# Four weight blocks instead of two share one row of 256-column products in the first token group of a two-layer MLP kernel

## The chip, the core and the metric

The kernel runs on one NeuronCore of one Trainium2 chip. The metric is the device time of one execution in microseconds, median of several executions. Five engines matter here: PE (TensorE, the matrix products), DVE (VectorE) and ACT (ScalarE) for elementwise work, SP for the DMA queue, and the DMA engines. Each engine works through its own list of instructions in the order in which the program issued them, and waits at an instruction until the semaphores that it needs have arrived.

## The reference

Attention with a sigmoid in place of the softmax, then two MLP layers, all in fp32:

```python
scores = scale * np.matmul(q, k.transpose(0, 1, 3, 2)) - np.log(S)
x = np.matmul(1.0 / (1.0 + np.exp(-scores)), v)      # 4 x 12 x 448 x 64 -> 1792 x 768
h = x @ w_in1; r = np.maximum(h, 0.0)                # 768 -> 2048
x = (s * (r * r) + b) @ w_out1                       # 2048 -> 768
h = x @ w_in2
g = np.maximum(h, 0.0) + alpha * np.minimum(h, 0.0)
out = g @ w_out2
```

The weights arrive as 64-bit floats and are turned into fp32 on the chip.

## The kernel before

After the attention (the first 131 us) the two MLP layers run as six passes, three token groups for each of the two layers: `PASSES`, (m, p). Group p = 0 has 768 tokens, groups 1 and 2 have 512. The first group therefore exists twice, as pass 0 and as pass 3, and the change touches these two passes alone.

A pass is 34 steps (`PER`), one weight block ("unit") each, numbered r = 0 to 33. Units 0 to 15 are "in": each makes one 128-row block of h out of six x blocks (six terms). Units 16 to 33 are "out": six output blocks dc, each cut into three units of 6, 5 and 5 terms (`OUT_CUTS`), which add into one accumulator; unit 16 reads g[0..5], unit 17 g[6..10], unit 18 g[11..15], and unit 19 is the first of the next output block.

Every fp32 operand is split into a high and a low part of a reduced precision, since a product of full precision is made of three: high x high, high x low, low x high. Per term and unit, `products` (L396) issues for p = 0: three products of 512 columns (L411 to L413), one of 512 columns that covers the last 256 tokens' high and low part with the high weight (L416), and one of 256 columns with the low weight (L402, the "short" one). The short ones of one unit stand in a row: an even unit has its row last, an odd unit its row first (`short_first`), so that the rows of units 2k and 2k+1 join to one row of 12 (or 11, or 10).

A step (loop at L564) issues, in this order: the stores of earlier steps, the products of unit n on PE, then the handling of the sums of unit n-1 (`evac`), then `split_unit(n+2)`, then `fetch(n+5)`, and in some steps a load or split of the next pass's x.

- `evac` of an "in" unit in group 0: ACT copies the sums out of PSUM (L437), DVE adds the second short part (L439), two more DVE operations (L447, L454 in layer 1; L461, L465 in layer 2), ACT casts the high part of g (L210), DVE subtracts for the low part (L217, two instructions). Of an "out" unit only the last cut of a block is handled (L437, L439 and a store).
- `split_unit(n+2)`: ACT casts the high part of the weights (L99), DVE subtracts for the low part (L102). Four buffers (`whl`).
- `fetch(n+5)`: either a load, or, for the units in `JUST` (the out units of pass 0 and 3), a conversion from 64 bits: ACT L141, DVE L147, L152, L155. So in passes 0 and 3 the steps 11 to 28 each carry a conversion.

Sums lie in PSUM in two pools of two buffers (`acc` for even blocks, `av` for odd ones), so unit k+4 takes the place of unit k.

Of the kernel before, what the change touches and what calls it, by code (L numbers as in the profile page):

```python
# [12 lines left out]
ALU = mybir.AluOpType  # L13
# [3 lines left out]
P = 128  # L17
OUT_CUTS = [(0, 6), (6, 11), (11, 16)]

PASSES = [(0, 0), (0, 1), (0, 2), (1, 0), (1, 1), (1, 2)]  # L20
N5 = 512
# [15 lines left out]
def tile_kernel(  # L37
# [13 lines left out]
    nc = tc.nc  # L51
    B, NPR, _, SKQ = kq.shape
# [3 lines left out]
    NK = NPR  # L56
    DM = NK * P
    NFC = w_in1.shape[0]
# [5 lines left out]
    TG = N5 + REST  # L64
    TOK = [TG, N5, N5]
    TOK0 = [0, TG, TG + N5]
    NCUT = len(OUT_CUTS)
    PER = NFC + NK * NCUT
# [22 lines left out]
    def t_tile(name):  # L91
        return tp.tile([P, TG], F32, tag="t", name=name)
# [4 lines left out]
    def split(hi, lo, src, eng_hi):  # L97
        if eng_hi == "A":
            nc.scalar.copy(hi, src)  # L99
        else:  # L100
            nc.vector.tensor_copy(hi, src)
        nc.vector.tensor_tensor(out=lo, in0=src, in1=hi.bitcast(F32), op=ALU.subtract)  # L102
# [17 lines left out]
    uses = [m * PER + j for m, _ in PASSES for j in range(PER)]  # L120
    r64, w32, wraw, whl = {}, {}, {}, {}
# [39 lines left out]
    def store32():  # L161
        for j, w in to_store:
            n = units[j][1]
            w32[j] = dram.tile([P, n], F32, tag=f"w{j}", name=f"w{j}")
            nc.sync.dma_start(out=w32[j], in_=w[:, :n])
        to_store.clear()

    def wraw_tile():
        return wrawp.tile([P, WMAX], F32, tag="wraw", name="wraw")

    def load32(i):
        n = units[uses[i]][1]
        t = wraw_tile()
        nc.sync.dma_start(out=t[:, :n], in_=w32[uses[i]])
        wraw[i] = t

    def split_unit(i):
        if i >= len(uses):
            return
        n = units[uses[i]][1]  # L180
        t = whlp.tile([P, 2, WMAX], F32R, tag="whl", name="whl")
        split(t[:, 0, :n], t[:, 1, :n], wraw.pop(i)[:, :n], "A")
        whl[i] = t
# [8 lines left out]
    def next64():  # L192
        if at64[0] < len(order64):
            load64(order64[at64[0]])
            at64[0] += 1


    x, x_dram, xr = {}, {}, {}
# [132 lines left out]
    def flush_stores():  # L331
        for dst, t in stores:
            nc.sync.dma_start(out=dst, in_=t)
        stores.clear()
# [6 lines left out]
    for _ in range(NWARM):  # L341
        for h in range(2):
            for j in range(2):
# [3 lines left out]
                    start=True, stop=True,  # L347
# [16 lines left out]
    for u in range(NU + 2):  # L364
# [7 lines left out]
        if u >= 2:  # L372
            q, c = order[u - 2]
# [5 lines left out]
        if u in conv_step:  # L379
            k = conv_step[u]  # L380
            w = ga[k][:, :WMAX]
# [11 lines left out]

    g, hp, op_ = {}, {}, {}

    def products(dst, p, terms, first, last, short_first):  # L396

        n = len(terms) - 1

        def short(start, stop):  # L400
            for k, (hi, lo, mv) in enumerate(terms):
                nc.tensor.matmul(  # L402
                    dst[:, N5:TG], lo, mv[:, 2 * N5 : N5 + TG],
                    start=start and k == 0, stop=stop and k == n, skip_group_check=True,
                )

        if p == 0 and short_first:
            short(first, False)
        for k, (hi, lo, mv) in enumerate(terms):
            end = last and k == n  # L410
            nc.tensor.matmul(dst[:, :N5], hi, mv[:, N5 : 2 * N5], start=first and k == 0, stop=False)  # L411
            nc.tensor.matmul(dst[:, :N5], hi, mv[:, :N5], start=False, stop=False)  # L412
            nc.tensor.matmul(dst[:, :N5], lo, mv[:, N5 : 2 * N5], start=False, stop=end)  # L413
        if p == 0:
            for k, (hi, lo, mv) in enumerate(terms):
                nc.tensor.matmul(  # L416
                    dst[:, N5 : 2 * N5], hi, mv[:, 2 * N5 :],
                    start=first and not short_first and k == 0,
                    stop=last and short_first and k == n,
                    skip_group_check=True,  # L420
                )
            if not short_first:
                short(False, last)

    def in_mm(p, fc, i):
        hp[fc] = (acc_tile, av_tile)[fc % 2]("hps").rearrange("p b s -> p (b s)")
        w = whl.pop(i)
        terms = []
        for kc in range(NK):
            cols = slice(kc * P, (kc + 1) * P)  # L430
            terms.append((w[:, 0, cols], w[:, 1, cols], x[kc]))
        products(hp[fc], p, terms, True, True, i % 2 == 1)

    def take(h, p, name):

# [39 lines left out]
        g[fc] = g_tile(fc).bitcast(F32R)[:, : 2 * TG]  # L475
        split_to(g[fc], t, 0, "A" if p == 0 else "V")

    def out_mm(p, dc, cut, i):
        c0, c1 = OUT_CUTS[cut]
        if c0 == 0:  # L480
            op_[dc] = (acc_tile, av_tile)[dc % 2]("ops").rearrange("p b s -> p (b s)")
        w = whl.pop(i)
        if i == len(uses) - 1:


            M = N5 // 2
            t = t_tile("o")[:, :N5]
            o2 = (acc_tile, av_tile)[(dc + 1) % 2]("ops2").rearrange("p b s -> p (b s)")
            for h in range(2):
                to = op_[dc] if h == 0 else o2  # L490
                for fc in range(c0, c1):
                    cols = slice((fc - c0) * P, (fc - c0 + 1) * P)
                    for k, o in ((0, N5), (0, 0), (1, N5)):
                        nc.tensor.matmul(  # L494
                            to[:, :M], w[:, k, cols],
                            g[fc][:, o + h * M : o + (h + 1) * M],
                            start=h == 1 and fc == c0 and k == 0 and o == N5,
                            stop=fc == c1 - 1 and k == 1,
                        )
                if h == 0:  # L500
                    nc.scalar.copy(t, op_[dc][:, :N5])
                else:
                    nc.vector.tensor_tensor(  # L503
                        out=t[:, M:], in0=o2[:, :M], in1=t[:, M:], op=ALU.add
                    )
                c = TOK0[p] + h * M
                nc.sync.dma_start(
                    out=out[dc * P : (dc + 1) * P, c : c + M], in_=t[:, h * M : (h + 1) * M]
                )
            return  # L510
        terms = []
        for fc in range(c0, c1):
            cols = slice((fc - c0) * P, (fc - c0 + 1) * P)
            terms.append((w[:, 0, cols], w[:, 1, cols], g[fc]))
        products(op_[dc], p, terms, c0 == 0, c1 == NFC, i % 2 == 1)

    def out_evac(m, p, dc):
        t = take(op_.pop(dc), p, "o")
        if m == 0:
            dst = x_store(1, p, dc)  # L520
        else:
            dst = out[dc * P : (dc + 1) * P, TOK0[p] : TOK0[p] + TOK[p]]
        stores.append((dst, t))

    def load_xr(key):
        xr[key] = t_tile("xr")[:, : TOK[key[1]]]
        nc.sync.dma_start(out=xr[key], in_=x_dram[key])

    def make_x(key):
        split_to(x_tile(key[2]), xr.pop(key), 0, "A")  # L530

    def evac(st):
        kind, m, p, c, cut = st
        if kind == "in":
            in_evac(m, p, c)
        elif cut == NCUT - 1:
            out_evac(m, p, c)

    def fetch(i):

        if i >= len(uses) or i in wraw:
            return
        j = uses[i]
        if j in JUST and j not in w32:
            w = wraw_tile()
            convert(j, w, "A")
            next64()
            wraw[i] = w
        else:
            load32(i)  # L550

    steps = []
# [6 lines left out]

    ahead = {PER + 2 + 4 * k: PER + k for k in range(NFC)}  # L560

    n_split, n_fetch = 2, 5
    pend = None
    for n, st in enumerate(steps):  # L564
        kind, m, p, c, cut = st
        o, r = divmod(n, PER)
        flush_stores()
        store32()
        if kind == "in":
            in_mm(p, c, n)  # L570
        else:
            out_mm(p, c, cut, n)
        if pend is not None:
            evac(pend)
        pend = st
        while n_split <= n + 2:
            split_unit(n_split)
            fetch(n_fetch)
            n_split += 1
            n_fetch += 1  # L580
        if kind == "out" and o + 1 < len(PASSES):

            kc, odd = divmod(r - NFC - 3, 2)
            if 0 <= kc < NK:
                key = (*PASSES[o + 1], kc)
                if odd:
                    make_x(key)
                else:
                    load_xr(key)
        if n in ahead:  # L590
            convert(ahead[n], t_tile("cw"), "A")
            next64()
# [42 lines left out]
```

## Time and profile before

| what | us |
|---|---|
| median of 3 runs | 1054.35 (1053.59 to 1054.69) |
| the profiled execution, its time | 1053.89 |
| its span, first to last instruction | 1052.1 |
| PE busy | 1047.9 |
| DVE busy | 594.8 |
| ACT busy | 448.5 |

The profile's page lists engines, slices of the span, DMA queues, the chain of work that ended last, and the costliest groups of instructions. Of a matmul the start is recorded and the end is modelled, so rows of matmuls are read from start to start: the time between the starts of two stretches is what the first one took. "idle before" in brackets is the time that the engine stood still ahead of an instruction, with what ended it.

### The profile page before, as it was taken

Reading aid. Unit: us, or ns where it says so; the run is one execution under the profiler, and the core shown is the slowest. Engines: PE = TensorE matmul, PEld = TensorE weight load, DVE = VectorE, ACT = ScalarE, POOL = GpSimd, SP = SyncE. Lnnn points to the kernel's source line nnn. Section 1 sums busy time; section 2 is a strip of 40 time slices with the busy share of each in tenths; the row PEclk is TensorE's granted clock in tenths of the full one; section 3 lists DMA queues with packets and bytes.
Section 4 is the critical chain, followed back from the end, with each engine's and each line's share of the span. In section 5 each row is a group of like instructions: output and inputs, shape, how many; then the busy total and the mean of one; then the engine's idle time right before and its main releaser. Section 6 shows DMA issues by size and latency. Waiting matters only on the chain.

```text
span 1052.1 us, 14275 instructions
## 1 busy us (share of the span) xinstructions
PE 1047.9 (100%) x5631; PEld 818.3 (78%) x5631; DVE 594.8 (57%) x881; ACT 448.5 (43%) x625; POOL 0.2 (0%) x4
## 2 busy tenths in 40 slices
PE   9999999999999999999999999999999999999998
PEld 4333388888888888888888888888888888888887
DVE  4765456687643775447745366786616652266521
ACT  6777733444332554335534333443314432344321
POOL 0000000000000000000000000000000000000000
PEclk9999999999999999999999999999999999999999
DMA  7787660048762545764566512468523235323330
GB/s 276 274 268 248 244 249 1 27 140 262 250 225 93 195 138 203 270 207 136 183 220 207 187 61 60 120 187 291 201 93 105 89 122 170 130 90 98 116 117 31
DMA packets 62131, 173.17 MB, mean 165 GB/s; under 512 B 8048, under 2 KB 10736, under 8 KB 62064
## 3 DMA queue, kind: packets, MB, share of 16 engines
q1 hardware_dynamic: 62064, 172.27, 49.1%
q8 instruction: 44, 0.72, 0.3%
q14 instruction: 23, 0.19, 0.1%
HBM read 132.92 MB, written 39.32 MB: 164 GB/s over the span
## 4 chain that ended last, share of the span: by engine, by line
PE 100%; DVE 0%; issue 0%; DVEq 0%
PE hps L411 12%; PE hps L412 12%; PE hps L413 12%; PE ops L411 12%; PE ops L413 12%; PE ops L412 12%; PE sc L281 6%; PE av L307 6%; PE ops L416 4%; PE hps L416 4%; PE hps L402 2%; PE ops L402 2%; PE ops L494 0%; PE wp L345 0%; DVE o L503 0%
## 5 line engine op out<-in xcount | busy, mean ns | idle before, releaser
L102 DVE TENSOR_TENSOR whl<-wraw,whl 128x768 fp32r<-128x768 f32 (+1 forms) x188 | 167.8, 903 | 130.8 <-ACT whl L99 130.1
L411 PE MATMUL hps<-x,whl 128*128 128x512 f32 x576 | 224.4, 390 | 0.0
L412 PE MATMUL hps<-x,whl 128*128 128x512 f32 x576 | 224.3, 389 | 0.0
L413 PE MATMUL hps<-x,whl 128*128 128x512 f32 x576 | 224.1, 389 | 0.0
L411 PE MATMUL ops<-g,whl 128*128 128x512 f32 x571 | 222.4, 389 | 0.0
L412 PE MATMUL ops<-g,whl 128*128 128x512 f32 x571 | 222.3, 389 | 0.0
L413 PE MATMUL ops<-g,whl 128*128 128x512 f32 x571 | 222.1, 389 | 0.0
L99 ACT CAST whl<-wraw 128x768 fp32r<-128x768 f32 (+1 forms) x188 | 146.7, 792 | 40.8 <-PE ops L413 25.5
L411 PEld LDWEIGHTS hps<-x,whl 128*128 128x128 f32 x576 | 108.2, 188 | 22.7 <-issue 0.7
L413 PEld LDWEIGHTS hps<-x,whl 128*128 128x128 f32 x576 | 108.1, 188 | 22.6
L412 PEld LDWEIGHTS hps<-x,whl 128*128 128x128 f32 x576 | 108.2, 188 | 21.8
L413 PEld LDWEIGHTS ops<-g,whl 128*128 128x128 f32 x571 | 107.2, 188 | 22.4
L412 PEld LDWEIGHTS ops<-g,whl 128*128 128x128 f32 x571 | 107.2, 188 | 21.7
L411 PEld LDWEIGHTS ops<-g,whl 128*128 128x128 f32 x571 | 107.2, 188 | 21.7
L291 ACT ACTIVATE ga<-sc,bias_t 128x896 f32<-128x896 f32 x84 | 84.5, 1008 | 33.2 <-PE sc L281 31.5
L217 DVE TENSOR_TENSOR g<-t,g 128x512 fp32r<-128x512 f32 (+1 forms) x128 | 77.2, 624 | 31.8 <-ACT g L210 28.6
L437 ACT COPY o<-ops 128x512 f32<-128x512 f32 (+1 forms) x35 | 23.1, 661 | 149.0 <-PE ops L413 92.1
L281 PE MATMUL sc<-ga 64*64 64x448 f32 x672 | 78.3, 544 | 0.0
L307 PE MATMUL av<-ga,ga 64*64 64x448 f32 x672 | 77.1, 536 | 0.0
L147 DVE SCALAR_TENSOR_TENSOR cva<-r,cva 128x768 f32<-128x768 f32 (+1 forms) x68 | 61.7, 908 | 6.0 <-ACT cva L141 4.7
L210 ACT CAST g<-t 128x768 fp32r<-128x768 f32 x32 | 26.7, 836 | 85.8 <-DVE t L465 42.0
L217 DVE TENSOR_TENSOR x<-xr,x 128x512 fp32r<-128x512 f32 (+1 forms) x36 | 22.7, 645 | 59.0 <-ACT x L210 59.0
(53 smaller groups left out, 817.3 us busy)
## 6 DMA issues: line engine op xcount, KB each, us to landing
wraw<-w SPq DMA_DIRECT2D x104, 384.0 KB, 3.1
r<-in_w_in SPq DMA_DIRECT2D x32, 768.0 KB, 5.1
r<-in_w_out SPq DMA_DIRECT2D x24, 640.0 KB, 5.1
wraw<-w SPq DMA_DIRECT2D x48, 320.0 KB, 3.5
ga<-in_qk SPq DMA_DIRECT2D x23, 448.0 KB, 5.2
r<-in_w_out SPq DMA_DIRECT2D x12, 768.0 KB, 5.4
w<-wraw SPq DMA_DIRECT2D x24, 320.0 KB, 5.7
ga<-in_vt SPq DMA_DIRECT2D x24, 256.0 KB, 5.3
```

Source lines behind the costliest of these rows:

```text
L99: nc.scalar.copy(hi, src)
L102: nc.vector.tensor_tensor(out=lo, in0=src, in1=hi.bitcast(F32), op=ALU.subtract)
L147: nc.vector.scalar_tensor_tensor(out=a.bitcast(F32), in0=hi.bitcast(F32), scalar=2.0**-112, in1=a.bitcast(F32), op0=ALU.mult, op1=ALU.max,)
L217: nc.vector.tensor_tensor(out=lo[:, a - o : e - o], in0=src[:, a - c0 : e - c0], in1=hi[:, a - c0 : e - c0].bitcast(F32), op=ALU.subtract,)
L281: nc.tensor.matmul(sc[h * D : (h + 1) * D, j, :S], kqt[q][rows, S + k0 : S + k0 + D], kqt[q][rows, :S], start=True, stop=True,)
L291: nc.scalar.activation(sg, sct.pop(u)[:, :, :S], AF.Sigmoid, bias=bias_t[:, 0:1], scale=QKSCALE)
L307: nc.tensor.matmul(avt[q][j * D : (j + 1) * D, h, :S], vtt[q][keys, j, c, :], sg[keys, j, :], start=first, stop=last,)
L402: nc.tensor.matmul(dst[:, N5:TG], lo, mv[:, 2 * N5 : N5 + TG], start=start and k == 0, stop=stop and k == n, skip_group_check=True,)
L411: nc.tensor.matmul(dst[:, :N5], hi, mv[:, N5 : 2 * N5], start=first and k == 0, stop=False)
L412: nc.tensor.matmul(dst[:, :N5], hi, mv[:, :N5], start=False, stop=False)
L413: nc.tensor.matmul(dst[:, :N5], lo, mv[:, N5 : 2 * N5], start=False, stop=end)
L416: nc.tensor.matmul(dst[:, N5 : 2 * N5], hi, mv[:, 2 * N5 :], start=first and not short_first and k == 0, stop=last and short_first and k == n,
```

## The change

In passes with p = 0, units are taken in fours by r. Units 4k and 4k+1 issue their long products, then follow the short products of both; units 4k+2 and 4k+3 have theirs right behind, ahead of their own long products. The order on PE is: long 0, long 1, short 0, short 1, short 2, short 3, long 2, long 3, in place of long 0, short 0, short 1, long 1, long 2, short 2, short 3, long 3. The last two units of a pass, r = 32 and 33, keep the old manner. The number and shape of the products stay as they are. In the step, `split_unit(n+2)` now stands ahead of `evac` for p = 0 (behind it for p > 0, as before); `fetch(n+5)` stays last. The very last unit has its own function, as before in another place.

```diff
+    def products(n):
+        p, r = steps[n][2], n % PER
+        if p > 0:
+            longs(unit_of(n), p, False)
+        elif r >= PER // 4 * 4:
+            odd = r % 2 == 1
+            for part in (odd, not odd):
+                if part:
+                    shorts(unit_of(n), odd)
+                else:
+                    longs(unit_of(n), p, odd)
+        elif r % 4 < 2:
+            longs(unit_of(n), p, False)
+            if r % 4 == 1:
+                shorts(unit_of(n - 1), False)
+                shorts(unit_of(n), False)
+        else:
+            if r % 4 == 2:
+                shorts(unit_of(n), True)
+                shorts(unit_of(n + 1), True)
+            longs(unit_of(n), p, True)
...
-        if kind == "in":
-            in_mm(p, c, n)
-        else:
-            out_mm(p, c, cut, n)
-        if pend is not None:
+        if n == len(uses) - 1:
+            last_mm(p, c, cut, n)
+        else:
+            products(n)
+        if p > 0 and pend is not None:
             evac(pend)
+        split_unit(n + 2)
+        if p == 0 and pend is not None:
+            evac(pend)
+        fetch(n + 5)
         pend = st
-        while n_split <= n + 2:
-            split_unit(n_split)
-            fetch(n_fetch)
-            n_split += 1
-            n_fetch += 1
```

`longs` holds the three products of 512 columns per term and, for p = 0, the fourth one (L411 to L416 of before), `shorts` the one of 256 (L402 of before); `unit_of(n)` takes the split weights of unit n and its accumulator when it is first asked for, which for a unit 4k+3 is now one step before its own.

## Rows read from the trace of the kernel before

**Rows 1.** The page: busy us by engine; chain that ended last, by engine.
```profile
PE 1047.9 (100%) x5631; PEld 818.3 (78%) x5631; DVE 594.8 (57%) x881; ACT 448.5 (43%) x625; POOL 0.2 (0%) x4
PE 100%; DVE 0%; issue 0%; DVEq 0%
```

**Rows 2.** Waits of PE in the whole span: us in total, times, longest.
```profile
PE wp L345 <- DVE bias_t L350: 1.0, 1, 1.0
```

**Rows 3.** Timeline of PE around one short row: start us, us, engine, line, operation, count.
```profile
160.24 1.52 PE L416 MATMUL hps<-x,whl 128*128 128x512 f32 x6
161.60 1.59 PE L402 MATMUL hps<-x,whl 128*128 128x256 f32 x12
163.03 0.40 PE L411 MATMUL hps<-x,whl 128*128 128x512 f32 x1
...
164.42 0.39 PE L411 MATMUL hps<-x,whl 128*128 128x512 f32 x1
```

**Rows 4.** Busy us and count by engine from 205.50 to 243.00 us, with clock.
```profile
205.50:243.00 37.50, 37.50 (x183) 31.72 (x182) 32.21 (x49) 16.32 (x23) 0.00 (x0) 1.00 0.49 144
```

**Rows 5.** Timeline of PE, pass 0: units 12, 16, short rows 10+11, 12+13, 18+19.
```profile
198.62 1.59 PE L402 MATMUL hps<-x,whl 128*128 128x256 f32 x12
...
205.52 0.39 PE L411 MATMUL hps<-x,whl 128*128 128x512 f32 x1
...
210.96 1.59 PE L402 MATMUL hps<-x,whl 128*128 128x256 f32 x12
...
230.20 0.39 PE L411 MATMUL ops<-g,whl 128*128 128x512 f32 x1
...
246.04 1.48 PE L402 MATMUL ops<-g,whl 128*128 128x256 f32 x11
```

**Rows 6.** Timeline of DVE, pass 0, from the sums of unit 10 on.
```profile
200.36 0.42 DVE L439 TENSOR_TENSOR t<-hps,t 128x256 f32<-128x256 f32 x1 [1.17 <-ACT t L437]
...
205.25 0.95 DVE L147 SCALAR_TENSOR_TENSOR cva<-r,cva 128x768 f32<-128x768 f32 x1
...
207.59 0.42 DVE L439 TENSOR_TENSOR t<-hps,t 128x256 f32<-128x256 f32 x1
...
214.48 0.42 DVE L439 TENSOR_TENSOR t<-hps,t 128x256 f32<-128x256 f32 x1
...
217.55 1.03 DVE L217 TENSOR_TENSOR g<-t,g 128x512 fp32r<-128x512 f32 x2 [0.94 <-ACT g L210]
218.50 0.95 DVE L102 TENSOR_TENSOR whl<-ga,whl 128x768 fp32r<-128x768 f32 x1
219.36 0.82 DVE L147 SCALAR_TENSOR_TENSOR cva<-r,cva 128x640 f32<-128x640 f32 x1
...
241.34 0.82 DVE L155 SCALAR_TENSOR_TENSOR wraw<-cva,wraw 128x640 uint32<-128x640 uint32 x1
242.08 0.95 DVE L102 TENSOR_TENSOR whl<-wraw,whl 128x768 fp32r<-128x768 f32 x1
```

**Rows 7.** Timeline of ACT, pass 0: copy of unit 12's sums, cast of unit 19's weights.
```profile
211.96 0.79 ACT L437 COPY t<-hps 128x768 f32<-128x768 f32 x1
...
239.59 0.82 ACT L99 CAST whl<-wraw 128x768 fp32r<-128x768 f32 x1
```

**Rows 8.** Timeline of PE, pass 3: the start of unit 12.
```profile
664.10 0.39 PE L411 MATMUL hps<-x,whl 128*128 128x512 f32 x1
```

**Rows 9.** Timeline of DVE, pass 3: sums of unit 12, split of unit 19.
```profile
672.90 0.42 DVE L439 TENSOR_TENSOR t<-hps,t 128x256 f32<-128x256 f32 x1
...
700.09 0.95 DVE L102 TENSOR_TENSOR whl<-wraw,whl 128x768 fp32r<-128x768 f32 x1
```

**Rows 10.** Timeline of PE at the start of the span: the first products of the attention.
```profile
1.05 2.84 PE L345 MATMUL wp<-idle 64*64 64x128 f32 x48 [1.05 <-DVE bias_t L350]
3.69 3.69 PE L281 MATMUL sc<-ga 64*64 64x448 f32 x24
...
7.96 0.92 PE L281 MATMUL sc<-ga 64*64 64x448 f32 x8
8.72 0.92 PE L307 MATMUL av<-ga,ga 64*64 64x448 f32 x8
```

More of the change, by code (lines that the diff above doesn't have):

```diff
@@ L394, in tile_kernel, with longs @@
     g, hp, op_ = {}, {}, {}
-    def products(dst, p, terms, first, last, short_first):
+    def longs(unit, p, short_first):
+        dst, terms, first, last = unit
         n = len(terms) - 1
[L400 to L408, printed above, removed]
         for k, (hi, lo, mv) in enumerate(terms):
@@ L421, in products, with shorts @@
                 )
[L422 to L432, printed above, removed]
+    def shorts(unit, short_first):
+        dst, terms, first, last = unit
+        n = len(terms) - 1
+        for k, (hi, lo, mv) in enumerate(terms):
+            nc.tensor.matmul(
+                dst[:, N5:TG], lo, mv[:, 2 * N5 : N5 + TG],
+                start=first and short_first and k == 0,
+                stop=last and not short_first and k == n,
+                skip_group_check=True,
+            )
@@ new lines, in tile_kernel, with unit_of @@
+    mms = {}
+    def unit_of(n):
+        if n not in mms:
+            kind, _, _, c, cut = steps[n]
+            w = whl.pop(n)
+            if kind == "in":
+                c0, c1, mv = 0, NK, x
+                hp[c] = (acc_tile, av_tile)[c % 2]("hps").rearrange("p b s -> p (b s)")
+                to = hp[c]
+            else:
+                (c0, c1), mv = OUT_CUTS[cut], g
+                if c0 == 0:
+                    op_[c] = (acc_tile, av_tile)[c % 2]("ops").rearrange("p b s -> p (b s)")
+                to = op_[c]
+            terms = []
+            for k in range(c0, c1):
+                cols = slice((k - c0) * P, (k - c0 + 1) * P)
+                terms.append((w[:, 0, cols], w[:, 1, cols], mv[k]))
+            mms[n] = to, terms, c0 == 0, c1 == (NK if kind == "in" else NFC)
+        return mms[n]
@@ L476, in in_evac, with last_mm @@
         split_to(g[fc], t, 0, "A" if p == 0 else "V")
-    def out_mm(p, dc, cut, i):
+    def last_mm(p, dc, cut, i):
         c0, c1 = OUT_CUTS[cut]
-        if c0 == 0:
-            op_[dc] = (acc_tile, av_tile)[dc % 2]("ops").rearrange("p b s -> p (b s)")
         w = whl.pop(i)
[L483 to L501, printed above, removed]
-                else:
-                    nc.vector.tensor_tensor(
-                        out=t[:, M:], in0=o2[:, :M], in1=t[:, M:], op=ALU.add
-                    )
-                c = TOK0[p] + h * M
-                nc.sync.dma_start(
-                    out=out[dc * P : (dc + 1) * P, c : c + M], in_=t[:, h * M : (h + 1) * M]
-                )
[L510 to L515, printed above, removed]
@@ new lines, in last_mm @@
+        M = N5 // 2
+        t = t_tile("o")[:, :N5]
+        o2 = (acc_tile, av_tile)[(dc + 1) % 2]("ops2").rearrange("p b s -> p (b s)")
+        for h in range(2):
+            to = op_[dc] if h == 0 else o2
+            for fc in range(c0, c1):
+                cols = slice((fc - c0) * P, (fc - c0 + 1) * P)
+                for k, o in ((0, N5), (0, 0), (1, N5)):
+                    nc.tensor.matmul(
+                        to[:, :M], w[:, k, cols],
+                        g[fc][:, o + h * M : o + (h + 1) * M],
+                        start=h == 1 and fc == c0 and k == 0 and o == N5,
+                        stop=fc == c1 - 1 and k == 1,
+                    )
+            if h == 0:
+                nc.scalar.copy(t, op_[dc][:, :N5])
+            else:
+                nc.vector.tensor_tensor(
+                    out=t[:, M:], in0=o2[:, :M], in1=t[:, M:], op=ALU.add
+                )
+            c = TOK0[p] + h * M
+            nc.sync.dma_start(
+                out=out[dc * P : (dc + 1) * P, c : c + M], in_=t[:, h * M : (h + 1) * M]
+            )
@@ L560, in tile_kernel @@
     ahead = {PER + 2 + 4 * k: PER + k for k in range(NFC)}
-    n_split, n_fetch = 2, 5
     pend = None
```

## The prediction

> **What bounds the kernel now.** I read the page first: PE is busy for 1047.9 of 1052.1 us and the chain that ended last is PE for 100% of the span [rows 1]. Next the waits: PE waits once, for 1.0 us at the very start, and never again [rows 2]. So the kernel is one unbroken row of products, and only two things move its time: the pace from start to start of the products, and any wait that PE is newly given. A wait of PE costs its full length, since nothing behind it is idle that could give it back. Then the timeline of PE round a short row, for the pace; then the timelines of DVE and ACT in passes 0 and 3, for how late the operands of a short row become ready. There the reader is to see one stretch, units 11 to 19 of either pass: DVE is busy 32.2 of 37.5 us [rows 4] and most of the rest is the pause of 0.94 us that each handling of sums has in its middle [rows 6], while ACT casts. In that stretch DVE carries a conversion in each step beside the sums and the split, and it is late.
>
> **What the merged rows save.** Six products of 512 columns take 161.60 - 160.24 = 1.36 us, 226.7 ns each, up to the first short one. Twelve short ones take 163.03 - 161.60 = 1.43 us, 119 ns each. The six products after the row take 164.42 - 163.03 = 1.39 us, 0.03 us more than six elsewhere [rows 3]. So leaving a row costs 0.03 us and entering it nothing. A pass has 17 rows now and 9 afterwards (eight of four units, one of two): 8 fewer in each of two passes, 16 x 0.03 = 0.5 us saved. If that 0.03 is only the rounding of the row, nothing is saved; it can hardly be a loss, since no product is added. I take 0.4.
>
> **What the new order asks for.** I put zero at the start of unit 12: 205.52 us in pass 0 [rows 5], 664.10 in pass 3 [rows 8]. A long part of six terms takes 210.96 - 205.52 = 5.44 us [rows 5]; one of five terms 20 x 0.2267 = 4.53; a short part six or five times 0.119, 0.72 or 0.60. New order on PE: long 12 at 0, long 13 at 5.44, short 12 from 10.88 to 11.60, shorts 13 to 15 until 13.74, long 14 and 15 until 24.64, long 16 until 30.08, long 17 until 34.61, short 16 to 35.33, short 17 to 35.93, short 18 to 36.53, and short 19 wants to start at 36.53. Before, the row of 18 and 19 started at 246.04 [rows 5], so short 19 at 246.04 + 0.60 - 205.52 = 41.12. The change asks for the low weights of unit 19 some 4.6 us earlier.
>
> **When they are ready.** Before, their split ended at 242.08 + 0.95 = 243.03 [rows 6], 37.51 after zero: 3.6 us early then. If nothing on DVE moved, PE would already wait 37.51 - 36.53 = 1.0 us. But DVE moves too. The sums of unit 12 used to be complete after its own short part, at 5.44 + 0.72 = 6.16; ACT copied them by 211.96 + 0.79 = 212.75, 7.23 after zero [rows 7], and DVE came to them, still behind with other work, only at 214.48, which is 8.96 [rows 6]. Now they are complete at 11.60. Where DVE isn't behind, it comes to a unit's sums 1.02 us after its last short product, copy and hand-over included: the row of units 10 and 11 began at 198.62 [rows 5], unit 10's part ended 0.72 later at 199.34, and DVE began at 200.36 [rows 6]. So it can't begin before 12.62. DVE stands before that instruction, and everything queued behind it stands too: the conversions of units 18 to 21, the sums of 13 to 15, the splits of 16 to 19. It loses 12.62 - 8.96 = 3.66 us. From the sums of unit 12 to the end of the split of unit 19 DVE worked 243.03 - 214.48 = 28.55 us [rows 6]; the list is the same afterwards but for one split, that of unit 15, which now precedes: 219.36 - 218.50 = 0.86 [rows 6]. So the split of unit 19 ends at 12.62 + 28.55 - 0.86 = 40.31, and PE waits 40.31 - 36.53 = 3.8 us. In pass 3: the same work took 700.09 + 0.95 - 672.90 = 28.14 [rows 9], so 12.62 + 28.14 - 0.86 = 39.90, a wait of 3.4. Of these waits the first part falls within short 18, whose last term reads the g of unit 15, a little late as well; it is covered by the wait for unit 19 and adds nothing. Both together: 7.2 us.
>
> DVE must be through with the earlier work by 12.62. The sums of unit 8 are complete at -24.64 + 11.60, and DVE starts on them 1.02 later, at -12.0. Sums and split without a conversion take 205.25 - 200.36 = 4.89, with one 207.59 - 200.36 = 7.23 or 214.48 - 207.59 = 6.89 [rows 6]. So unit 9 is begun at -7.1, 10 at -2.2, 11 at 5.0, and the split of unit 15 is over at 11.9. This is 0.7 before the sums of 12 and 1.1 before short 15 asks for it at 13.03. So that row doesn't wait by this sum, but with little to spare.
>
> **The split ahead of the sums.** It issues one cast on ACT and one subtraction on DVE and no DMA, and it passes only the handling of one unit's sums; the loads and conversions of `fetch` stay behind both, so on SP's queue the order stays. Without it the split of unit 4k+3 would stand behind sums that are complete only in the row that needs it, so it is needed; its own cost is the g of the unit, later by 0.86, which is in the sum above. In steps without a conversion DVE has the time: 4.89 of work for a unit of 6.16. In the out steps sums come only at every third unit, and the next row there, units 20 to 23, asks for the split of unit 23 some 20 us after the wait, with four steps of split and conversion (7.23 - 4.89 + 0.86 = 3.2 each) to be done: nothing. PSUM: unit k+4 takes the buffer of unit k, and long 16, at 24.64, finds that of unit 12 read by 12.62 + 0.42 [rows 6]: nothing. Passes with p > 0 keep order and products: nothing.
>
> Would a queue let later work pass the waiting instruction? The row: the cast of unit 19's weights was over at 239.59 + 0.82 = 240.41 [rows 7], yet DVE's subtraction began at 242.08, right behind L155 [rows 6]. DVE did not take it earlier. The Trainium skill, "TensorE: Matmul & The Clock Gate", table at its head, calls the queues of ScalarE and VectorE strict FIFO, and says TensorE may pull weight loads, by Part 3 of that page (The mechanism) not matmuls, ahead. By that rule the sum stands; were long 18 to pass short 19 on PE, the wait would vanish. No row of before shows PE at such a wait.
>
> **The sum.** The profiled execution took 1053.89, its span 1052.1: 1053.89 - 0.4 + 7.2 = 1060.7. The median of the runs is 0.46 above the profiled one, so 1061.1 on that scale. Each wait can err by a microsecond (the DVE cycle with a conversion varies from 6.89 to 7.23 [rows 6], four of them lie in between): 1059.1 to 1063.1.
>
> **The rivals.**
> (a) Not slower: PE doesn't wait. Then the rows' saving is left, 1054.35 - 0.4 = 1053.95, within 0.2%. It decides at one point: the split of unit 19 must end by 36.53. That would need the DVE to be 3.8 us quicker in a stretch where it idles about 0.94 us per unit, or matmuls that pass one another. Against it: even unmoved, that split comes 1.0 late. 7%; of real gain, through a cheaper long row than the rows show, 3%, at about 1051.
> (b) The clock falls in the wait. PE has no pause in this trace after 1.05 us, and the granted clock is given as 1.00 throughout [rows 4], so it doesn't show. The nearest rows are PE's start: 24 products of the scores took 3.69 us, where later 8 take 8.72 - 7.96 = 0.76, or 2.28 for 24 [rows 10]: 1.4 lost there, and 1.3 in the 3.69 - 1.05 = 2.64 us of products before, if they too ran at half pace. At up to 2.7 for each of two waits, 1061.1 + 5.4 = 1066.5. For: the pauses are microseconds long. Against: they are shorter than the work between them by far. 10%. The Trainium skill's page named above, Part 1, says that the low clock is the default and activity lifts it, which goes with these rows; no row shows a fall.
> (c) More waits: the split of unit 15 is late as well (it has 1.1 to spare), or a converted weight in the out units is. 1 to 4 us more, 1062 to 1065, say 1063.6. 10%.
> My forecast has 70%.
>
> **How the numbers follow.** Likeliest 1061.1. The range must hold 8 in 10: the forecast's 1059.1 to 1063.1 widened by 0.9 below for a median that differs, and above by (c) and most of (b): 1058.2 to 1065.8. What a measurement of this kernel can tell from no change is about 0.2%, 2.1 us. Faster 0.03; same 0.07; slower 0.90.
>
> **What would show it.** In the profile of after: two waits of PE, one in each of passes 0 and 3, at the short products of unit 18 or 19, about 242 to 246 and 704 to 708 us, on DVE L102 (or on g); PE busy otherwise without a gap; rows of 24, 23 or 21 short ones at 119 ns; DVE idle ahead of the sums of unit 12 at about 218. It would be wrong if PE waits nowhere (then DVE had slack that I don't see), if waits stand in every row (then the splits of 4k+3 are late everywhere), or if the pace of 226.7 ns changes.

## The result, and the profile after

The changed kernel takes 1064.95 us (median of 5, 1063.15 to 1066.74) where the kernel before takes 1054.38: 1.0106 times as long, 95% interval 1.0094 to 1.0117. It is slower by 10.6 us. The profiled execution took 1064.41, its span is 1062.6, 10.5 more than before; the working below explains these 10.5.

The page of after: busy us by engine, and the chain that ended last, by engine.

```profile
PE 1051.4 (99%) x5631; PEld 839.9 (79%) x5631; DVE 593.3 (56%) x881; ACT 446.9 (42%) x625; POOL 0.2 (0%) x4
PE 94%; DVE 2%; issue 2%; ACT 1%; ACTq 0%; DVEq 0%
```

The number of products is the same as in [rows 1], 5631, yet PE is busy 3.5 us longer, and 6% of the chain now runs over other engines. So there are two things to look for: waits of PE, and products that became slower. The waits of PE in the whole span of after (total us, times, longest):

```profile
PE ops L419 <- DVE whl L102: 7.0, 2, 3.6
PE wp L345 <- DVE bias_t L350: 1.0, 1, 1.0
```

Against [rows 2] there are two new ones, both at short products (L419) and both on the DVE's subtraction for the weights (L102). The timeline of PE round the first of them (start us, us, engine, line, operation, count):

```profile
240.10 2.24 PE L419 MATMUL ops<-g,whl 128*128 128x256 f32 x16
245.98 1.03 PE L419 MATMUL ops<-g,whl 128*128 128x256 f32 x6 [3.63 <-DVE whl L102]
246.80 0.63 PE L402 MATMUL ops<-g,whl 128*128 128x512 f32 x1
247.24 0.63 PE L403 MATMUL ops<-g,whl 128*128 128x512 f32 x1
...
250.19 0.39 PE L404 MATMUL ops<-g,whl 128*128 128x512 f32 x1
250.42 0.39 PE L402 MATMUL ops<-g,whl 128*128 128x512 f32 x1
```

The sixteen are the short products of units 16, 17 and 18; short 19 follows the sixteenth. The sixteenth started at 241.96 (the row's 240.10 + 2.24, less the 0.28 that a short product is given), so short 19 wanted to start 0.12 later, at 242.08, and started at 245.98: a wait of 3.9 us from start to start (the bracket counts from the modelled end and so gives less). In pass 3 the same, a wait of 3.6 by the same reckoning:

```profile
704.14 2.07 PE L419 MATMUL ops<-g,whl 128*128 128x256 f32 x16
709.61 0.95 PE L419 MATMUL ops<-g,whl 128*128 128x256 f32 x6 [3.40 <-DVE whl L102]
710.39 0.40 PE L402 MATMUL ops<-g,whl 128*128 128x512 f32 x1
...
714.50 0.39 PE L404 MATMUL ops<-g,whl 128*128 128x512 f32 x1
```

Behind the wait in pass 0 the products of 512 columns start 0.43 us apart instead of 0.227, and take 0.63 instead of 0.39. The granted clock of those stretches (window, its length, busy us and count of PE, PEld, DVE, ACT, POOL, then the clock as a share of 2.4 GHz, DMA share, GB/s):

```profile
246.00:250.00 4.00, 4.00 (x14) 3.32 (x15) 3.17 (x5) 1.47 (x3) 0.00 (x0) 0.59 0.98 281
...
706.00:710.00 4.00, 0.60 (x5) 0.42 (x5) 3.86 (x7) 2.32 (x4) 0.00 (x0) 1.00 0.31 68
710.00:714.50 4.50, 4.50 (x16) 3.61 (x15) 3.76 (x6) 1.56 (x3) 0.00 (x0) 0.62 0.93 294
```

During the wait in pass 3 the clock is still given as 1.00; then it stands near 0.6 as a mean, that is, most of the stretch at the lower of its two levels (1.2 GHz), before it returns to 2.4. What this costs: from 245.98 to 250.42 PE made six short and nine long products in 4.44 us; at full pace they take 6 x 0.119 + 9 x 0.2267 + 0.03 = 2.78. So 1.7 us are lost behind the wait. In pass 3, six short and eleven long products took 714.50 - 709.61 = 4.89 us; at full pace they take 3.24, so 1.7 are lost there too.

Sum: 3.9 + 3.6 of waits, 2 x 1.7 of lower clock, less 0.3 for the merged rows (shown below) is 10.6; the span grew by 10.5. These 3.4 us of lower clock are those of the profiled execution. The five executions have mean granted clocks of 0.997 (1063.15 and 1064.41 us), 0.996 (1064.95) and 0.993 (1066.24 and 1066.74): the slower they are, the more of the time was at the lower level.

### The profile page after: what moved, and what is told of

Read it like the earlier page. It is cut to its first block, busy times and chain, and to the rows that moved or that the text cites. A ratio compares the mean times of both kernels' runs of the same rounds, so it can differ in the third digit from the quotient of the medians.

```text
span 1062.6 us, 14277 instructions
## 1 busy us (share of the span) xinstructions
PE 1051.4 (99%) x5631; PEld 839.9 (79%) x5631; DVE 593.3 (56%) x881; ACT 446.9 (42%) x625; POOL 0.2 (0%) x4
## 4 chain that ended last, share of the span: by engine, by line
PE 94%; DVE 2%; issue 2%; ACT 1%; ACTq 0%; DVEq 0%
PE ops L402 12%; PE hps L402 12%; PE ops L404 12%; PE ops L403 12%; PE hps L403 12%; PE hps L404 12%; PE sc L281 6%; PE av L307 6%; PE ops L407 4%; PE hps L407 4%; PE ops L419 2%; PE hps L419 2%; ACT g L210 1%; DVE whl L102 0%; DVE t L503 0%
## 5 line engine op out<-in xcount | busy, mean ns | idle before, releaser
L102 DVE TENSOR_TENSOR whl<-wraw,whl 128x768 fp32r<-128x768 f32 (+1 forms) x188 | 167.8, 902 | 140.8 <-ACT whl L99 140.0
L402 PE MATMUL hps<-x,whl 128*128 128x512 f32 x576 | 224.3, 389 | 0.0
L402 PE MATMUL ops<-g,whl 128*128 128x512 f32 x571 | 223.7, 392 | 0.0
L402 PEld LDWEIGHTS hps<-x,whl 128*128 128x128 f32 x576 | 108.1, 188 | 22.9 <-issue 0.7
L402 PEld LDWEIGHTS ops<-g,whl 128*128 128x128 f32 x571 | 108.0, 189 | 22.2
L281 PE MATMUL sc<-ga 64*64 64x448 f32 x672 | 124.9, 539 | 0.0
L307 PE MATMUL av<-ga,ga 64*64 64x448 f32 x672 | 124.5, 537 | 0.0
L281 PEld LDWEIGHTS sc<-ga 64*64 64x64 f32 x672 | 48.3, 133 | 40.3 <-issue 33.1
L307 PEld LDWEIGHTS av<-ga,ga 64*64 64x64 f32 x672 | 49.8, 132 | 19.4 <-issue 15.4
```

Source lines behind the costliest of these rows:

```text
L281: nc.tensor.matmul(sc[h * D : (h + 1) * D, j, :S], kqt[q][rows, S + k0 : S + k0 + D], kqt[q][rows, :S], start=True, stop=True,)
L307: nc.tensor.matmul(avt[q][j * D : (j + 1) * D, h, :S], vtt[q][keys, j, c, :], sg[keys, j, :], start=first, stop=last,)
```

## The experiments

Theory A is that of the prediction, with the clock added: PE waits because short 19 is asked for before DVE has split its weights, DVE being late because it stands at the sums of unit 12; and the wait brings the clock down. The rivals: the longer rows of short products bring the clock down by themselves (theory B); the moved split is a part of the loss; something other than DVE's list ends the wait. Each run is set against executions of the kernel before from the same session, whose median is 1053.81 us for the first four runs below and 1053.78 for the others.

### Rows of two for units 16 to 19 only

```diff
-        elif r >= PER // 4 * 4:
+        elif r >= PER // 4 * 4 or NFC <= r < NFC + 4:
```

> The changed kernel, but units 16 to 19 of passes 0 and 3 keep the old rows of two (rows per pass: 10 instead of 17 before and 9 after). Theory A (PE waits because short 19 is asked for before DVE has split its weights, and the clock falls because of that wait): short 19 is asked for 41.1 us after the start of unit 12, its split ends at 40.3, so PE waits nowhere, the granted clock stays 1.000, and 14 rows fewer at 0.015 to 0.03 us each give a span of 1051.7 to 1051.9, a median of 1054.0. Theory B (the clock falls because of the longer unbroken rows of 256 columns): 8 rows of 21 to 24 are still there per pass less one, so the clock still falls, mean below 0.999, and the time is 1056 or more. Theory C (the whole stretch of units is late, not unit 19 alone): a wait of 1 us or more stands in another row, 1056 to 1060.

Measured: 1053.63 us (11 runs) against 1053.81, ratio 0.9999 (0.9990 to 1.0008), clock 1.000. Its waits of PE, then the timelines of PE and of DVE at units 18 and 19:

```profile
PE wp L345 <- DVE bias_t L350: 1.0, 1, 1.0
```

```profile
246.18 1.48 PE L419 MATMUL ops<-g,whl 128*128 128x256 f32 x11
```

```profile
245.09 0.95 DVE L102 TENSOR_TENSOR whl<-wraw,whl 128x768 fp32r<-128x768 f32 x1
```

Short 19 is the sixth of those eleven and starts near 246.18 + 5 x 0.119 = 246.78; the split of its weights is done at 246.04, 0.7 us ahead (0.8 expected). DVE is as late as in the changed kernel; only PE asks later. Theory B and theory C (the whole stretch is late) fall: seven rows of 21 to 24 remain in each pass, and neither a fall of the clock nor another wait is left. The whole loss hangs on these four units.

### The split ahead of the sums, alone

The kernel before with this edit only (`split_unit` and `evac` change places where p = 0):

```diff
-        if pend is not None:
+        if p > 0 and pend is not None:
             evac(pend)
+        split_unit(n + 2)
+        if p == 0 and pend is not None:
+            evac(pend)
+        fetch(n + 5)
         pend = st
-        while n_split <= n + 2:
-            split_unit(n_split)
-            fetch(n_fetch)
...
```

> The kernel before, with only the split of weights put ahead of the handling of sums in passes 0 and 3; rows of two as before. Theory A: the split's place alone costs nothing where rows are short, since the g of a unit gets later by only 0.86 us and nothing waits for it: no wait of PE, 1054.4, ratio 1.000. Rival: the moved split is itself part of the 10 us, through sums that are handled later: a wait at unit 18 or 19 and 1056 to 1059.

Measured: 1053.84 us (10 runs), ratio 1.0003 (0.9994 to 1.0012), clock 1.000, no wait of PE beyond the first. The place of the split costs nothing by itself.

### The rows of four, alone

```diff
-        if p > 0 and pend is not None:
+        if pend is not None:
             evac(pend)
         split_unit(n + 2)
-        if p == 0 and pend is not None:
-            evac(pend)
         fetch(n + 5)
```

> The changed kernel with the split left behind the handling of sums, as before: only the rows of four. Theory A: in each four of in units the split of unit 4k+3 stands behind the sums of unit 4k, which are complete only inside the row; from there DVE needs 1.02 + 4.9 us, the row gives it 1.4, so PE waits some 4.5 us at four rows of each pass, about 1 at one row of the out units, and hardly at unit 19: about 38 us of waits, and with a fall of the clock of up to 1.7 us at each of eight, 1092 to 1106. Rival (the place of the split makes no difference): 1065, as the changed kernel.

Measured, one execution: 1106.78 us, 0.8 above the upper end that I had put down, clock 0.988. Its waits of PE:

```profile
PE hps L419 <- DVE whl L102: 35.4, 8, 4.5
PE ops L419 <- DVE whl L102: 2.2, 2, 1.1
PE wp L345 <- DVE bias_t L350: 1.0, 1, 1.0
```

Eight waits of about 4.5 us at rows of "in" units and two of 1.1 at rows of "out" units, as worked out. So the two parts of the change belong together: without the split's new place every four of "in" units waits. The timeline of DVE after the first row shows the chain that the split of unit 3 stood behind:

```profile
144.47 0.42 DVE L477 TENSOR_TENSOR t<-hps,t 128x256 f32<-128x256 f32 x1 [10.27 <-ACT t L475]
...
147.54 1.03 DVE L217 TENSOR_TENSOR g<-t,g 128x512 fp32r<-128x512 f32 x2 [0.94 <-ACT g L210]
148.48 0.95 DVE L102 TENSOR_TENSOR whl<-ga,whl 128x768 fp32r<-128x768 f32 x1
```

The sums of unit 0 from 144.47, then the subtraction for unit 3 from 148.48; PE went on at 149.49. The span grew by 52.9 us. Waits are 39.2 of it, from start to start (37.6 in the view); what is left, with the 0.3 that the merged rows save some 14, goes with the clock. In the 3.5 us from where PE goes on the clock is 0.51 to 0.61 behind each of the eight long waits and 1.00 behind both short ones; eight times the 1.7 us of the changed kernel is 13.6. The window behind the first wait:

```profile
149.50:153.00 3.50, 3.50 (x13) 2.92 (x14) 2.49 (x4) 1.44 (x2) 0.00 (x0) 0.61 0.26 99
```

### DVE work taken out of the list ahead of unit 19

Two of the three DVE operations of the conversion (L147, L155) are left out for units 18 to 21, 20 alone, or 20 and 21 of passes 0 and 3:

```diff
-            convert(j, w, "A")
+            convert(j, w, "A", i % PER in (18, 19, 20, 21))
...
+        if not light:
+            nc.vector.scalar_tensor_tensor(
+                out=a.bitcast(F32), in0=hi.bitcast(F32), scalar=2.0**-112, in1=a.bitcast(F32),
...
+        if not light:
+            nc.vector.scalar_tensor_tensor(
+                out=u, in0=a, scalar=3, in1=u,
...
```

Units 18 to 21:

> The changed kernel with two of the three DVE operations of the conversion left out for units 18 to 21 of passes 0 and 3 (their weights are then not the true ones); rows and order as changed. It takes 6.2 us of DVE work out of the list ahead of the split of unit 19, which was 3.9 and 3.6 us late. Theory A: no wait of PE, granted clock 1.000, 1054.1 (span 1051.8). Theory B (the clock falls by the rows themselves): no wait, but a clock of about 0.997 and 1057.5. Rival C (ACT or the loads set the split's end, not DVE): the wait stays at 2 us or more, 1060 to 1065.

Measured: 1053.53 us (10 runs), ratio 0.9997 (0.9988 to 1.0006), clock 1.000, no wait of PE but the first. The rows are those of the changed kernel, all eight of four units in each pass, and the loss is gone: rival B, the rows themselves, falls, and so does this run's rival C, that ACT or the loads set the end of the split. This kernel also shows what the rows save when nothing waits. The first product of pass 0 and that of pass 1, in the kernel before and then in this one:

```profile
131.34 0.50 PE L411 MATMUL hps<-x,whl 128*128 128x512 f32 x1
...
328.94 0.39 PE L411 MATMUL hps<-x,whl 128*128 128x512 f32 x1
```

```profile
131.59 0.50 PE L404 MATMUL hps<-x,whl 128*128 128x512 f32 x1
...
329.02 0.39 PE L404 MATMUL hps<-x,whl 128*128 128x512 f32 x1
```

197.60 us against 197.43: 0.17 for 8 rows fewer, 0.02 a row, 0.3 us in both passes.

Unit 20 alone:

> The changed kernel with two of the three DVE operations of the conversion left out for unit 20 alone in passes 0 and 3 (its weights are then not the true ones): 1.47 us less on DVE ahead of the split of unit 19. Theory A: the waits shrink by that much, to 2.4 and 2.1 us. If the clock falls behind them as behind the longer ones: 1053.5 + 4.5 + 3.4 = 1061.4; if waits of this length leave the clock alone: 1058.0. Rival (DVE isn't what ends the wait): waits as in the changed kernel, 1064.

Measured: 1059.52 us (4 runs), ratio 1.0054 (1.0039 to 1.0069), clock 0.998. The row ahead of short 19 and short 19 in the two passes, and the clock behind it:

```profile
240.84 1.00 PE L421 MATMUL ops<-g,whl 128*128 128x256 f32 x7
244.06 1.42 PE L421 MATMUL ops<-g,whl 128*128 128x256 f32 x6 [2.22 <-DVE whl L102]
...
703.24 1.12 PE L421 MATMUL ops<-g,whl 128*128 128x256 f32 x8
706.16 0.95 PE L421 MATMUL ops<-g,whl 128*128 128x256 f32 x6 [1.81 <-DVE whl L102]
```

```profile
244.00:248.00 4.00, 3.94 (x13) 3.41 (x14) 3.29 (x5) 1.58 (x3) 0.00 (x0) 0.57 0.97 284
706.00:710.00 4.00, 3.84 (x20) 3.34 (x21) 3.19 (x6) 1.56 (x4) 0.00 (x0) 1.00 0.92 298
```

From start to start the waits are 2.4 and 2.0 us, 1.5 and 1.6 less than in the changed kernel, for 1.47 us of DVE work taken away: it is DVE's list, nearly one for one. In this execution the clock fell behind the wait of 2.4 and not behind that of 2.0, and the time lies between the two that I had written down, for two falls and for none: 1058.0 and one fall of 1.7 is 1059.7.

Units 20 and 21:

> The same for units 20 and 21: 2.94 us less on DVE. Theory A: waits of 1.0 and 0.6 us; the waits of 1.1 us in the run with the rows of four alone had no fall of the clock behind them, so none here: 1053.5 + 1.6 = 1055.1, clock 1.000. Rival (DVE isn't what ends the wait): 1064.

Measured: 1054.90 us (10 runs), ratio 1.0011 (1.0001 to 1.0021), clock 1.000; two waits, 1.0 us together:

```profile
PE ops L421 <- DVE whl L102: 1.0, 2, 0.7
```

As expected: the waits go on shrinking, and behind such short ones the clock stays.

### The kernel before, with a late split

Rows of two and the old order; only the split of unit 19 ends late, since its subtraction is made ten times.

```diff
-        split(t[:, 0, :n], t[:, 1, :n], wraw.pop(i)[:, :n], "A")
+        raw = wraw.pop(i)[:, :n]
+        split(t[:, 0, :n], t[:, 1, :n], raw, "A")
+        if i in (19, 3 * PER + 19):
+            for _ in range(9):
+                nc.vector.tensor_tensor(
+                    out=t[:, 1, :n], in0=raw, in1=t[:, 0, :n].bitcast(F32), op=ALU.subtract
+                )
```

> The kernel before, rows of two and old order, but DVE repeats the subtraction for unit 19's weights nine times more in passes 0 and 3 (9 x 0.87 = 7.8 us; the result is the same). It had 3.6 us to spare in pass 0 and 4.2 in pass 3. Theory A: PE waits 4.2 and 3.6 us at short 19, about as in the changed kernel, and the clock falls behind each wait for up to 1.7 us of loss: 1053.9 + 7.8 + 3.4 = 1065. Theory B (the clock falls through the longer rows of 256 columns): the waits alone, clock 1.000, 1061.7.

Measured: 1068.48 us (4 runs), ratio 1.0140 (1.0125 to 1.0155), clock 0.995. Its waits of PE, DVE's repeats, and the clock behind the second wait:

```profile
PE ops L408 <- DVE whl L186: 10.1, 2, 5.3
```

```profile
242.68 8.90 DVE L186 TENSOR_TENSOR whl<-wraw,whl 128x768 fp32r<-128x768 f32 x9
```

```profile
716.60:722.00 5.40, 5.39 (x16) 4.53 (x17) 5.18 (x8) 2.13 (x3) 0.00 (x0) 0.50 0.57 152
```

The repeats took 8.9 us and not the 7.8 I had put (0.99 each from start to start, not 0.87), so the waits are a good microsecond longer than expected, 5.3 and 4.8 in the view and 5.5 and 4.9 from start to start, and the time is 1068 and not 1065. But the point is made: with the old rows and the old order, a split that is late by some microseconds gives both the wait and the fall of the clock. Theory B's 1061.7 was reckoned with waits of 7.8 in all; with the 10.4 that they measured it gives 1053.9 + 10.4 = 1064.3 at a clock of 1.000, and 1068.48 at 0.995 rules that out too. The rows of four matter in that they ask earlier.

### The change in pass 0 alone

```diff
-        elif r >= PER // 4 * 4:
+        elif r >= PER // 4 * 4 or n >= PER:
...
-        if p > 0 and pend is not None:
+        if o > 0 and pend is not None:
             evac(pend)
         split_unit(n + 2)
-        if p == 0 and pend is not None:
+        if o == 0 and pend is not None:
             evac(pend)
```

> The changed order in pass 0 alone; pass 3 keeps rows of two and the split behind the sums. Theory A: the two passes are independent, so one wait of 3.9 us and one fall of the clock: 1053.9 + 3.9 + 1.7 - 0.2 = 1059.3, and pass 3 as in the kernel before. Rival (the cost lies in one of the passes only, or pass 0's lateness carries on): the whole 10 us, or none.

Measured: 1059.57 us (4 runs), ratio 1.0056 (1.0041 to 1.0071), clock 0.998 or 0.997: about half of the whole loss, as expected. One wait; and the clock behind it:

```profile
245.83 1.62 PE L419 MATMUL ops<-g,whl 128*128 128x256 f32 x6 [3.64 <-DVE whl L102]
247.25 0.63 PE L402 MATMUL ops<-g,whl 128*128 128x512 f32 x1
...
251.82 0.40 PE L404 MATMUL ops<-g,whl 128*128 128x512 f32 x1
```

```profile
245.80:252.00 6.20, 6.17 (x18) 5.19 (x19) 5.42 (x8) 1.97 (x3) 0.00 (x0) 0.53 0.93 310
```

The wait has the length of that in the changed kernel, 3.9 us, but here the clock was already low at the first short product behind it (six of them take 1.42 us, 0.78 behind the wait in pass 3 of the changed kernel), and it stayed low until 251.8. Six short and eleven long products took 251.82 - 245.83 = 5.99 us where full pace is 3.24: 2.7 lost and not 1.7. With the wait, less 0.2 for the rows, that is 6.4, as the span grew (1058.5 against 1052.1). The lost time behind a like wait thus differs from one execution to the next, which goes with the wide spread of the changed kernel's executions, 3.6 us, where the run with rows of two for units 16 to 19 spreads over 0.7.

## Why the prediction was right, and what it left out

**What bounds the kernel, and the place.** Right: PE had no slack, and the two waits stand at short 19 in passes 0 and 3, on L102, and nowhere else.

**The merged rows.** I took 0.4 us at 0.03 a row; it is 0.3 at 0.02. Within a row the second short product starts 113 ns after the first and the others 120 apart, in the kernel before as in the changed one, so entering a row gains 7 ns of the 28 that leaving it costs; my reading "entering it nothing" left that out. The rows are of 24, 22 and 21 short products, not of 24, 23 and 21 as I wrote. Small either way.

**When the weights are ready.** The chain held to a tenth of a microsecond. The timeline of DVE in pass 0 of after, split of unit 15, sums of unit 12, split of unit 19:

```profile
216.50 0.95 DVE L102 TENSOR_TENSOR whl<-ga,whl 128x768 fp32r<-128x768 f32 x1
218.15 0.42 DVE L477 TENSOR_TENSOR t<-hps,t 128x256 f32<-128x256 f32 x1 [0.70 <-ACT t L475]
...
244.88 0.95 DVE L102 TENSOR_TENSOR whl<-wraw,whl 128x768 fp32r<-128x768 f32 x1
```

Forecast, from the start of unit 12 at 205.52: split of unit 15 over by 11.9, that is 217.42, measured 217.45; sums of 12 begun at 12.62, 218.14, measured 218.15; split of 19 over at 40.31, 245.83, measured 245.83. The bracket of 0.70 is what DVE stands still: it is short, since DVE comes to the sums late anyway, with its earlier work put off in the same manner. Where the answering row of [rows 6] was at 214.48, it is now 3.67 later. The waits, 3.8 and 3.4 by the forecast, measured 3.9 and 3.6.

**The split ahead of the sums.** Right that it is needed and costs nothing: alone it changes nothing, and without it each four of "in" units waits 4.5 us.

**The queues.** Right as taken: PE did not take long 18 ahead of short 19. The products of 512 columns came only at 246.80, behind the row. The Trainium skill, "TensorE: Matmul & The Clock Gate", Part 3, The mechanism, says that matmuls keep their order while weight loads may be pulled ahead; the trace agrees as to the matmuls.

**The clock.** This is the term that was missing. I gave it a chance of 10% and no share in the likeliest sum, on the ground that the pauses are short against the work between them. That ground was wrong: one pause of a few microseconds brought the clock down although 240 us and more of unbroken work lay ahead of it. Each of the two cost 1.7 us in the profiled execution, 3.4 of the 10.5. The bound that I had from PE's start, up to 2.7 each, was about right: 2.7 is what the single wait cost in the run with pass 0 alone. My own sign of being wrong, that the pace of 226.7 ns changes, came up: behind both waits these products started 0.43 us apart for some microseconds. The forecast of 1061.1 plus 3.4 is 1064.5, and the measured median is 1064.95. So the sum that I called likeliest gave 6.7 us of the 10.6, and its own bounds, 1059.1 to 1063.1, missed. The stated range, 1058.2 to 1065.8, held the median by 0.85 us and only because it reached towards this rival and towards further waits, which didn't come; two of the five executions lie above it. That part of the success is luck.

**The other rivals.** No wait: out, the split of unit 19 was over at 245.83, 3.8 us after the point that decides, 205.52 + 36.53. More waits: none; the split of unit 15 was over at 217.45, and short 15 came at 218.50, so it had 1.05 us to spare where I had worked out 1.1.

## What to carry to other kernels

In a kernel whose PE never pauses, a reordering of products has to be costed by when each operand is asked for, against the queues of the engines that make it: an operand that had 3.6 us to spare was asked for 4.6 us earlier, and an in-order engine that stands at a sum which is complete later carries its delay to everything behind. Where the gain is a few tenths of a microsecond and a wait of PE costs its length and, for each wait of 2.4 us or more in these runs, a stretch at about half pace, merge only where the makers of the operands have room (here, outside the units that follow the conversions). A wait should be priced with the clock, not only with its length.

## What the runs showed of the hardware

The granted clock fell behind single waits of PE of a few microseconds, in a kernel that is otherwise busy without a gap: from start to start, behind all eight of 4.5 to 4.6 us, all three of 3.6 to 3.9, both of 4.9 and 5.5, and one of 2.4; not behind one of 2.0, nor behind four of 1.3 us or less. PE then ran at the lower level, 0.43 us for a product of 512 columns instead of 0.227, although it was busy again. The Trainium skill, "TensorE: Matmul & The Clock Gate", Part 1, What's actually happening, says that the throttled state is the default and activity releases it. The trace agrees: the clock is 0.50 behind the second wait of the late split and 1.00 at 255.2 to 258.0 us, between its two waits. What decides between the wait of 2.4 that brought the clock down and that of 2.0 that didn't, and whether the loss is 1.7 or 2.7, was seen in single executions only and stays open.

A subtraction on DVE that writes the same tile again took 0.99 us each in a row of nine, where the same operation among others advances DVE by 0.87. Why is not shown.
